# Two VectorE steps of an attention-and-MLP kernel moved one unit later: the row sums of batch 2, and half of the last chunk's S2

## The chip, the cores and the metric

The kernel runs on one core of a Trainium2 chip. The metric is the time on the device in microseconds (us), lower is better. It is quoted as the median of repeated runs; besides, there is one execution recorded by the hardware profiler, from which all durations of single instructions come.

## The reference

Eight batches with eight heads, 576 rows and 64 columns each go through a linear attention, and its result, seen as 4608 tokens of 512 numbers, through a two-layer network with a SiLU between the layers:

```
q_s = softmax(q) over the 64 columns of each row
k_s = softmax(k) over the 576 rows
kv  = k_s^T v                      (64 x 64 for each head)
x   = q_s kv, heads side by side   (4608 x 512)
h   = x w_in                       (4608 x 2048)
out = (h * sigmoid(h)) w_out       (4608 x 512)
```

The row sum of exp(q) and the product with its reciprocal, "row sums" and "normalising" below, are the softmax of q.

## The kernel before, in words

**Tiling.** The tokens are cut into nine chunks of 512 (`TCH`), numbered t = 0 to 8, the batches into eight of 576, numbered b. Chunk 0 is done with plain products. From chunk 1 on, both layers are done by a Strassen-Winograd scheme with one level: seven products of half size in the order `ORDER` = 1, 2, 6, 5, 7, 4, 3 instead of eight, paid for with sums on VectorE. For the first layer `group` (line 363) does one of the seven for one half (g = 1 or 0) of the columns of `w_in`; its sums of the inputs are `xs_op` (L330, on the tokens) and `ws_op` (L320, on the weights, once). The products 1, 6, 7 and 4 go to PSUM bank pair 0, the products 2, 5 and 3 to another pair (6 in chunk 1, 2 later). ScalarE copies bank pair 0 into the SBUF tiles H0, H1, H2 (`group_snap`), VectorE adds the other pair to them (`group_add`, L354), and ScalarE takes the SiLU into `GT` (`group_silu`, L359). The sum of H0 belongs to product 2 and empties the pair that product 5 overwrites. The sum of H2 belongs to product 7; product 3 then adds to the same pair and so has to wait until that sum has read it. For the second layer `s_op` (L451) forms S1 to S4 from `GT`, and `t_op` (L461) forms T1 to T4 from `w_out` once; `prod` (L477) does the products. S2 is one of the operands of product 6, and S4 is formed from S2.

**Batches.** For batch b, ScalarE takes `exp_q` and `exp_k` (L108, L113), VectorE sums the rows and takes the reciprocals (`qsum`, L156 and L158), GpSimd multiplies (`qnorm`, L163) and casts v (`vcast`, L91). SP's DMA queue then transposes the normalised q (`q_transpose`, L173). TensorE forms kv (`kv`, L195), VectorE divides it (`kvcopy`, L206 and L208), and TensorE forms x for the chunk (`xt_mm`, L234). The batch has two halves of four heads, numbered cc.

**What sets the order.** The order is written out by hand. The list `units` holds pieces of TensorE's work; `plan(u, f)` puts a step f just before unit u, and steps of the same unit run in the order in which they were planned. The whole is issued as one sequence (L826), and each engine works off its own instructions in this order, each waiting for its operands. So a step that is moved by one unit moves on its engine past whatever that unit issues there.

**Around batch 2's row sums.** Unit numbers b1 + n count from `b1`, the first unit after chunk 0's first layer. Units b1+9 to b1+22 mix the seven products of chunk 1 and g = 1 with chunk 0's plain second layer (`mm2_plain`, L414): product 1, mm2, product 2, product 6, mm2, product 5, mm2, product 7, mm2, mm2, product 4, mm2, product 3, mm2. Then follow eight plain pieces of chunk 1's first layer (`mm1`, L285), among which kv and xt of batch 2 are placed. At b1+10 come the four `xs_op` with `ws_op(1, 0)` and `exp_q(2, 0)`; at b1+11 `qsum(2, 0, 0)`, `qsum(2, 0, 1)` and `qnorm(2, 0)`; at b1+13 `exp_q(2, 1)` and `ws_op(2, 0)`; at b1+14 `exp_k(2, 0)` and the row sums and normalising of the other half; at b1+17 `exp_k(2, 1)` and the two casts of v; at b1+18 `t_op(2)`; at b1+24 `t_op(4)` and `ws_op(3, 0)`; at b1+25 `kv_both(2)`. The row sums of half 0 thus stand on VectorE's queue ahead of the sum of H0.

**Around the last chunk.** Chunk 8's first layer takes 28 units that end at `begin[NCH]`, mixed with chunk 7's second layer; after them comes chunk 8's second layer alone. The unit `begin[NCH] - 7` is product 7 of group g = 0, whose VectorE work is the sum of H2. Ahead of it stand `s_op(7, 4)` and one half, four of the eight blocks, of chunk 8's S2. The other half of S2 is formed after `begin[NCH]`.

Of the kernel before, what the change touches and what calls it, by code (L numbers as in the profile page):

```python
# [17 lines left out]
def kernel(  # L18
# [9 lines left out]
    nc = tc.nc  # L28
# [12 lines left out]
    NCH = NT // TCH  # L41
# [60 lines left out]
    def half(t, cc):  # L102
        return t[:, :, cc * 128:(cc + 1) * 128].rearrange("p j (g d) -> p j g d", d=D)

    def exp_q(b, cc, g0=0, g1=2):
        if "eq" not in st[b]:
            st[b]["eq"] = ap.tile([128, J, NG * D], BF16, name="eq")
        nc.scalar.activation(  # L108
            out=half(st[b]["eq"], cc)[:, :, g0:g1], in_=jgd(b, "qt", cc)[:, :, g0:g1], func=ACT.Exp
        )  # L110
# [34 lines left out]
    def new_zq(b):  # L145
        if "zq" not in st[b]:
            st[b]["zq"] = ap.tile([128, 2, J, 2], FP32, name="zq", bufs=2)
            st[b]["rzq"] = ap.tile([128, 2, J, 2], FP32, name="rzq", bufs=2)

    def qsum(b, cc, gs=None):  # L150
        new_zq(b)
        z, e = st[b]["zq"][:, cc], half(st[b]["eq"], cc)
        if gs is None:
            nc.vector.reduce_sum(out=z, in_=e, axis=AX.X)  # L154
        else:
            nc.vector.reduce_sum(out=z[:, :, gs], in_=e[:, :, gs, :], axis=AX.X)  # L156
        if gs != 0:
            nc.vector.reciprocal(out=st[b]["rzq"][:, cc], in_=z)  # L158

    def qnorm(b, cc, eng):  # L160
        e = half(st[b]["eq"], cc)
        r = st[b]["rzq"][:, cc]
        eng.tensor_tensor(  # L163
            out=e, in0=e, in1=r[:, :, :, None].to_broadcast([128, J, 2, D]), op=ALU.mult
        )
# [273 lines left out]
    def blk(t, kh, th):  # L439
        return GTS[t % 2][:, kh * HF:(kh + 1) * HF, th * HT:(th + 1) * HT]  # L440

    def s_op(t, i, f0=0, f1=HF):
        in0, in1, op = {
            1: (blk(t, 0, 1), blk(t, 1, 1), ALU.add),
            2: (SS[1], blk(t, 0, 0), ALU.subtract),
            3: (blk(t, 0, 0), blk(t, 0, 1), ALU.subtract),
            4: (blk(t, 1, 0), SS[2], ALU.subtract),
        }[i]
        f = slice(f0, f1)
        o = blk(t, 0, 1) if i == 3 else SS[i]  # L450
        nc.vector.tensor_tensor(out=o[:, f], in0=in0[:, f], in1=in1[:, f], op=op)  # L451
# [171 lines left out]
    def plan(u, f):  # L623
        at.setdefault(u, []).append(f)
# [7 lines left out]
    begin = {1: len(units)}  # L632
# [83 lines left out]
    begin[NCH] = len(units)  # L716
    last = NCH - 1
    plan(begin[NCH] - 11, lambda: s_op(last, 1, 4, 8))
    plan(begin[NCH] - 7, lambda: s_op(last, 2, 4, 8))
    plan(begin[NCH], lambda: (s_op(last, 1, 0, 4), s_op(last, 2, 0, 4), s_op(last, 3)))  # L720
    plan(begin[NCH] + 6, lambda: s_op(last, 4))

# [48 lines left out]
    b1 = begin[1]  # L771
# [26 lines left out]
    plan(b1 + 10, lambda: (xs_op(1, 1), ws_op(1, 0)))  # L798
    plan(b1 + 10, lambda: (xs_op(1, 2), xs_op(1, 3), xs_op(1, 4)))
    plan(b1 + 10, lambda: exp_q(2, 0))  # L800
    plan(b1 + 11, lambda: (qsum(2, 0, 0), qsum(2, 0, 1), qnorm(2, 0, nc.gpsimd)))
    plan(b1 + 13, lambda: exp_q(2, 1))
    plan(b1 + 14, lambda: exp_k(2, 0))
    plan(b1 + 14, lambda: (qsum(2, 1, 0), qsum(2, 1, 1), qnorm(2, 1, nc.gpsimd)))
# [56 lines left out]
```

## Time and profile before

| | |
|---|---|
| median of 14 runs | 263.47 us (262.94 to 264.06) |
| the profiled execution, its own time | 262.99 us |
| span in the profile | 261.2 us (1.79 us lie around it) |
| VectorE busy | 208.8 us (80%) |
| ScalarE busy | 187.6 us (72%) |
| GpSimd busy | 65.6 us (25%) |
| granted TensorE clock | 0.995 of full |

Lines as "L355" are lines of the kernel; h is one of H0 to H2, WS what `ws_op` forms, T what `t_op` forms, S what `s_op` forms, zq the row sums, rzq their reciprocals, eq the exponentials of q, PS the PSUM. In a timeline each line has the start, the length, the engine, the line with its operation, what it writes and reads, and in brackets how long the engine had been idle and what ended that. PE is TensorE, PEld its weight load, DVE VectorE, ACT ScalarE, POOL GpSimd.

A group of four mm2 matmuls takes the place of about 0.86 us on TensorE and one product of chunk 1 about 0.77 us, as their starts follow on each other. On VectorE, a sum h of chunk 1 takes 1.03 us, a `ws_op` 0.68 us, a half `s_op` 0.69 us and a `t_op` 1.22 us, each when nothing holds it up; the two row sums of one half take 1.41 us together and the reciprocal 0.27 us. On GpSimd one `qnorm` takes 2.11 us and one cast 1.15 us.

### The profile page before, as it was taken

The page shows a single profiled execution, that of the slowest core. Times are in us where ns is not written, and L with a number is a line of the kernel's source. Part 1 is how long each engine was busy: PE and PEld are TensorE (multiplying, and loading weights), DVE is VectorE, ACT ScalarE, POOL GpSimd, SP SyncE. Part 2 cuts the span into 40 slices and gives each one's busy share as a digit, 9 for nine tenths or more (in the row PEclk, how much of TensorE's full clock was granted, in tenths as well). Part 3 has the DMA queues.
Part 4 walks back from the last instruction along what each step waited for, and adds up shares of the span by engine and source line. Part 5 has one row for each costly group of instructions (what it writes and reads, how often), then busy time and mean ns, then how long its engine had stood idle before and what let it go on. Part 6 is the DMA issues. An engine that isn't in the chain of part 4 may idle for free.

```text
span 261.2 us, 6409 instructions
## 1 busy us (share of the span) xinstructions
PE 252.0 (96%) x2732; PEld 203.5 (78%) x2732; DVE 208.8 (80%) x268; ACT 187.6 (72%) x212; POOL 65.6 (25%) x63
## 2 busy tenths in 40 slices
PE   8899999799999999999999999999999999999992
PEld 3467656556888888888888888888888888888881
DVE  2867897998997999799979997999798548855832
ACT  4767977798994799479957995799573848484610
POOL 1663790460360306030603060306000000000003
PEclk9999999999999999999999999999999999999998
DMA  6999999669999586957694869530433003300624
GB/s 233 345 198 297 298 319 335 252 124 385 312 342 216 143 231 211 214 141 204 240 250 104 218 228 210 142 84 3 90 81 82 3 0 83 80 3 1 141 63 121
DMA packets 35964, 45.89 MB, mean 176 GB/s; under 512 B 16208, under 2 KB 21008, under 8 KB 35936
## 3 DMA queue, kind: packets, MB, share of 16 engines
q1 hardware_dynamic: 29568, 33.69, 47.3%
q0 software_dynamic: 6128, 11.60, 17.1%
q8 instruction: 21, 0.34, 0.5%
q10 hardware_dynamic: 240, 0.20, 0.2%
q14 instruction: 7, 0.06, 0.1%
HBM read 36.70 MB, written 9.44 MB: 177 GB/s over the span
## 4 chain that ended last, share of the span: by engine, by line
PE 84%; DMA 5%; issue 4%; POOL 2%; ACT 2%; DVE 2%; POOLq 0%; ACTq 0%
PE PS L477 37%; PE PS L377 34%; DMA qt<-in_q_dram 5%; PE PS L414 5%; PE PS L285 2%; PE PS L234 2%; PE PS L195 2%; POOL W L554 1%; PE PS L267 1%; POOL out_dram L740 1%; DVE zq L156 1%; ACT sg L256 0%; ACT eq L108 0%; PE PS L181 0%; DVE h L355 0%
## 5 line engine op out<-in xcount | busy, mean ns | idle before, releaser
L355 DVE TENSOR_TENSOR h<-PS,h 128x1024 f32<-128x1024 f32 (+1 forms) x45 | 53.9, 1198 | 12.2 <-ACT h L89 6.3
L477 PEld LDWEIGHTS <-GT 128*128 128x128 f16 x512 | 49.6, 98 | 6.9 <-issue 1.2
L377 PEld LDWEIGHTS <-WS 128*128 128x128 f16 x480 | 46.8, 98 | 7.9 <-issue 2.3
L477 PE MATMUL PS<-W,GT 128*128 128x256 f16 x384 | 49.1, 273 | 0.0
L377 PE MATMUL PS<-XS,WS 128*128 128x256 f16 (+1 forms) x360 | 46.3, 272 | 1.5 <-DVE h L355 1.5
L361 ACT ACTIVATE GT<-h 128x1024 f16<-128x1024 f32 (+1 forms) x45 | 46.1, 1047 | 0.3 <-DVE h L355 0.3
L89 ACT COPY h<-PS 128x1024 f32<-128x1024 f32 (+1 forms) x35 | 35.1, 1004 | 14.5 <-PE PS L377 14.1
L163 POOL TENSOR_TENSOR eq<-eq,rzq 128x1152 bf16<-128x1152 bf16 x13 | 27.5, 2117 | 55.2 <-DVE rzq L158 52.4
L477 PEld LDWEIGHTS <-S 128*128 128x128 f16 x384 | 37.2, 98 | 5.2 <-issue 1.0
L377 PEld LDWEIGHTS <-W 128*128 128x128 f16 x360 | 34.7, 98 | 4.7 <-issue 0.2
L477 PE MATMUL PS<-T,S 128*128 128x256 f16 x256 | 32.7, 273 | 0.0
L377 PE MATMUL PS<-XT,W 128*128 128x256 f16 (+1 forms) x240 | 29.5, 272 | 0.0
L361 ACT ACTIVATE GT<-PS 128x1024 f16<-128x1024 f32 (+1 forms) x15 | 15.3, 1017 | 18.9 <-PE PS L377 18.9
L91 POOL CAST vaug<-vt 128x1152 bf16<-128x1152 f32 x12 | 14.8, 1240 | 43.8 <-DMA vt<-in_v_dram 35.4
L108 ACT ACTIVATE eq<-qt 128x1152 bf16<-128x1152 f32 (+1 forms) x18 | 19.1, 1059 | 2.8 <-DMA qt<-in_q_dram 2.6
L740 POOL DMA_DIRECT2D out_dram<-ow x5 | 2.7, 546 | 72.5 <-DVE ow L725 72.5
L113 ACT ACTIVATE ek<-kt 128x1152 bf16<-128x1152 f32 x16 | 18.4, 1154 | 1.5 <-DMA kt<-in_k_dram 1.5
L154 DVE TENSOR_REDUCE zq<-eq 128x18 f32<-128x1152 bf16 x12 | 16.1, 1345 | 4.0 <-ACT eq L108 4.0
L477 PE MATMUL PS<-W,S 128*128 128x256 f16 x128 | 16.5, 273 | 0.0
L497 DVE SCALAR_TENSOR_TENSOR ow<-PS,sc 128x512 f32<-128x512 f32 x7 | 4.8, 692 | 14.5 <-ACT sc L493 14.5
L267 PE MATMUL PS<-XT,W 128*128 128x288 f16 x128 | 16.0, 286 | 0.1
L414 PE MATMUL PS<-W,GT 128*128 128x512 f16 x64 | 15.6, 379 | 0.0
(79 smaller groups left out, 345.2 us busy)
## 6 DMA issues: line engine op xcount, KB each, us to landing
out_dram<-ow SPq DMA_DIRECT2D x64, 128.0 KB, 2.4
qt<-in_q_dram SPq DMA_DIRECT2D x12, 576.0 KB, 4.6
kt<-in_k_dram SPq DMA_DIRECT2D x12, 576.0 KB, 5.4
vt<-in_v_dram SPq DMA_DIRECT2D x12, 576.0 KB, 5.4
qt<-in_q_dram POOLq DMA_DIRECT2D x4, 576.0 KB, 10.2
kt<-in_k_dram POOLq DMA_DIRECT2D x4, 576.0 KB, 13.5
vt<-in_v_dram POOLq DMA_DIRECT2D x4, 576.0 KB, 13.0
W<-in_moe_w_out_dram POOLq DMA_DIRECT2D x4, 512.0 KB, 14.6
```

The costliest lines, as they stand in the source:

```text
L89: eng.copy(out=o, in_=i)
L91: eng.tensor_copy(o, i)
L108: nc.scalar.activation(out=half(st[b]["eq"], cc)[:, :, g0:g1], in_=jgd(b, "qt", cc)[:, :, g0:g1], func=ACT.Exp)
L113: nc.scalar.activation(out=half(ek, cc), in_=jgd(b, "kt", cc), func=ACT.Exp)
L154: nc.vector.reduce_sum(out=z, in_=e, axis=AX.X)
L163: eng.tensor_tensor(out=e, in0=e, in1=r[:, :, :, None].to_broadcast([128, J, 2, D]), op=ALU.mult)
L267: nc.tensor.matmul(out=PS[:, WIDE[fb] + n, 0:S // 2], lhsT=W1[:, c, fb * 128:(fb + 1) * 128], rhs=XTS[0][:, c, n * (S // 2):(n + 1) * (S / ...
L355: nc.vector.tensor_tensor(out=four(t, i), in0=group_bank(t, True), in1=four(t, i), op=ALU.add)
L361: nc.scalar.activation(out=group_out(t, f, n), in_=x, func=ACT.Silu, scale=1.0 / XS)
L377: nc.tensor.matmul(out=PS[:, bank + p // 2, (p % 2) * HT:(p % 2) * HT + width(t)], lhsT=a[:, c, p * 128:(p + 1) * 128], rhs=bb[:, c, 0:wid ...
L414: nc.tensor.matmul(out=PS[:, 2 + tb, :], lhsT=GTS[t % 2][:, fc, tb * 128:(tb + 1) * 128], rhs=W2[:, fc, :], start=(fc == 0), stop=(fc == N ...
L477: nc.tensor.matmul(out=PS[:, bank, m * HN:(m + 1) * HN], lhsT=a[:, fc, m * 128:(m + 1) * 128], rhs=bb[:, fc, :], start=(first and fc == 0) ...
```

## The change

Both edits change one number, the unit ahead of which a step stands.

```diff
-    plan(begin[NCH] - 7, lambda: s_op(last, 2, 4, 8))
+    plan(begin[NCH] - 6, lambda: s_op(last, 2, 4, 8))
...
-    plan(b1 + 11, lambda: (qsum(2, 0, 0), qsum(2, 0, 1), qnorm(2, 0, nc.gpsimd)))
+    plan(b1 + 12, lambda: (qsum(2, 0, 0), qsum(2, 0, 1), qnorm(2, 0, nc.gpsimd)))
```

In the second edit the two row sums and the reciprocal of batch 2's half 0 go on VectorE's queue from before the sum of H0 (product 2, unit b1+11) to behind it. `qnorm(2, 0)` moves with them, but unit b1+11 issues nothing on GpSimd. In the first edit half of chunk 8's S2 goes from before the sum of H2 (product 7) to behind it. No instruction is added or removed, and no DMA is moved.

## Prediction

> **What bounds the kernel now.** First the page's busy times, then TensorE's waits, then the engines' busy time by stretches (columns: length, then busy us of PE, PEld, DVE, ACT, POOL, granted clock, DMA share, GB/s).
>
> ```profile
> PE 252.0 (96%) x2732; PEld 203.5 (78%) x2732; DVE 208.8 (80%) x268; ACT 187.6 (72%) x212; POOL 65.6 (25%) x63
> ```
> ```profile
> PE PS L377 <- DVE h L355: 1.5, 1, 1.5
> ```
> ```profile
> 41.80:48.00 6.20, 4.66 (x41) 3.54 (x38) 4.79 (x10) 5.60 (x6) 1.25 (x1) 1.00 1.11 337
> 48.00:62.70 14.70, 14.70 (x170) 8.45 (x168) 14.53 (x18) 11.81 (x17) 6.17 (x4) 1.00 0.70 208
> ...
> 219.90:243.70 23.80, 23.76 (x218) 21.14 (x217) 16.14 (x20) 15.53 (x18) 0.00 (x0) 1.00 0.18 40
> ```
>
> TensorE bounds. The one wait of over 1.2 us that it has is for a sum h; it lies between 41.8 and 48, where 1.54 us of 6.20 are idle. Behind it TensorE has no gap that I can find up to 241.8, so a us saved at 46 is kept to the end unless something else comes late. In 48 to 62.7, however, VectorE is busy 14.53 of 14.70: that is what will come late.
>
> The chain of waits says who makes the sum late:
>
> ```profile
> 43.65 1.18 ACT eq L108
> 44.83 0.02 issue
> 44.85 1.43 DVE zq L156 x2
> 46.27 0.02 issue
> 46.30 0.27 DVE rzq L158
> 46.56 0.96 DVE h L355
> 47.52 0.04 issue
> 47.56 0.93 PE PS L377 x8
> ```
>
> VectorE stands 0.98 us for the exponential, sums rows, takes the reciprocal, and only then adds H0, though product 2 had ended at 44.39 and ScalarE's copy of H0 at 43.76. TensorE's product 5 waits for this.
>
> **The first edit in time: the row sums.** With the sum of H0 first, it starts 0.04 behind product 2's end (the sum at 243.06 starts 0.04 after its product's end at 243.02): 44.43, and ends at 45.46. Product 5 follows four mm2 matmuls that start at 44.99, and such a group takes 0.86 of TensorE (52.45 to 53.31), so it is due at 45.85, not 47.56. **The stall is worth 47.56 - 45.85 = 1.71 us**; the sum has 0.39 to spare.
>
> What is late next? TensorE is now 1.71 ahead, and whatever it meets must be too. These rows of the timeline decide (VectorE and GpSimd; left-out rows are marked), with one from the view of the tile vaug (shortest, median and longest duration in ns):
>
> ```profile
> 46.48 1.03 DVE L355 TENSOR_TENSOR h<-PS,h 128x896 f32<-128x896 f32 x1
> 46.75 2.11 POOL L163 TENSOR_TENSOR eq<-eq,rzq 128x1152 bf16<-128x1152 bf16 x1 [7.26 <-DVE rzq L158]
> ...
> 47.42 1.98 DVE L328 TENSOR_TENSOR WS<-WS,W 128x1024 f16<-128x1024 f16 x1
> ...
> 51.09 1.09 DVE L355 TENSOR_TENSOR h<-PS,h 128x896 f32<-128x896 f32 x1
> 51.17 2.12 POOL L163 TENSOR_TENSOR eq<-eq,rzq 128x1152 bf16<-128x1152 bf16 x1 [2.32 <-ACT h L89]
> ...
> 52.10 2.27 DVE L461 TENSOR_TENSOR T<-W,T 128x2048 f16<-128x2048 f16 x1
> ```
> ```profile
> L91 POOL CAST vaug<-vt x2: 1153/1652/2152, 53.2 to 55.3; 128x1152 bf16<-128x1152 f32 x2
> ```
>
> The ws_op at 47.42 took 1.98 instead of 0.69: it ended at 49.40, that is 0.54 after GpSimd's normalising had ended at 48.86. The t_op at 52.10 took 2.27 instead of 1.22, ending 1.08 after the next normalising. The other way round, the first cast of v took 2.15 instead of 1.15: it had started behind that t_op and ended 1.01 after it. The sum h at 51.09, with one operand in PSUM, took 1.09 beside GpSimd, so it is not held. So the two engines exclude each other in operations that read two SBUF operands, and the first to start wins. The Trainium skill says so too and speaks against the change (SBUF — State Buffer, section SBUF: two separate sides: a pair of ports shared by VectorE and GpSimd is an exclusive lock, kept for the whole instruction): the edit puts ws_op(2, 0) directly behind the reciprocal that releases GpSimd's normalising. The sum depends on who is first.
>
> VectorE's queue after the edit: sum of H0 44.43; row sums from 45.37 (+0.94, as from 46.48 to 47.42; their exponential ended at 44.82); reciprocal 46.82 to 47.09 (+1.45, as 44.85 to 46.30). The next instruction starts 0.18 after a reciprocal's start (46.30 to 46.48), and GpSimd 0.45 after it (46.30 to 46.75). So ws_op starts at 47.00, GpSimd would at 47.27. Here a rule is less kind than the row: VectorE: DVE Perf Modes, section The DRAIN you can't avoid, lets the next operation start only when the pipe is empty, at 47.09 then. By the row VectorE leads by 0.27, by the rule by 0.18. I take VectorE first.
>
> Case A, VectorE first: ws_op 47.00 to 47.69; normalising ends 49.7 (ws_op's end, plus 2.11, less some 0.14 of start-up as with the cast). Second row sums 47.6 to 49.04, reciprocal to 49.34. Product 7 now starts at 47.48 and ends at 48.41; ScalarE has its exponential done at 48.40 and copies H2 to 49.36. Sum of H2 49.40 to 50.48; product 3, which needs it, is due at 53.31 - 1.71 = 51.60: no stall. Second normalising 49.65 to 51.77; t_op(2), queued at 50.41, is held to 51.77 + 1.08 = 52.85. The casts come behind it: 53.86 and 54.95. kv is due at 56.55 - 1.71 = 54.84, its second half, which needs the second cast, at 55.20: no stall. Sum of H1 to 53.85, an output copy to 54.46, t_op(4) queued at 54.37 and held by the second cast to 54.95 + 1.08 = 56.03; ws_op(3, 0) from 55.95, kvcopy's reciprocal 0.60 later at 56.55, its products end at 57.24 (58.09 to 58.78 before); xt can start 0.12 later as before (58.78 to 58.90): 57.36. It is due at 58.90 - 1.71 = 57.19. **So 0.17 is given back.** Covers: kt's second half lands 11.7 after its issue at 36.9, at 48.6, its exponential starts at 49.25; the v halves land at 50.15 and 51.66, before their casts; the transpose is issued at 51.8, lands 4.7 later at 56.5, due 57.19. ScalarE's table load and SiLU follow that exponential 1.7 earlier than before. If these covers were gone, each us of lateness would cost at most itself, less the margin (0.6 for kt).
>
> First edit: 1.71 - 0.17 = **1.54 gained**. Bounds of the unknown, who gets the ports: 1.71 gained if nothing comes late, 0.57 lost if GpSimd is first (below).
>
> **The second edit: half of S2.** Near the end:
>
> ```profile
> 240.11 0.69 DVE L451 TENSOR_TENSOR S<-S,GT 128x1024 f16<-128x1024 f16 x1
> 240.72 1.22 DVE L355 TENSOR_TENSOR h<-PS,h 128x1024 f32<-128x1024 f32 x1
> 240.81 0.86 PEld L477 LDWEIGHTS <-S 128*128 128x128 f16 x8
> 240.91 1.04 PE L477 MATMUL PS<-W,S 128*128 128x256 f16 x8
> ...
> 241.99 1.03 PE L377 MATMUL PS<-XT,WS 128*128 128x256 f16 x8
> ```
>
> Products follow each other by 0.87 here, so product 3 was due at 240.91 + 0.87 = 241.78 and came at 241.99, 0.05 after the sum of H2 had ended at 241.94. Without the half S2 the sum starts at 240.11 and ends at 241.33: **0.21 gained**. Behind it the half S2 runs 241.25 to 241.94, and the next on the queue, the output copy that started at 241.85, starts where it did. S2 is first read by product 6 at 247.22: 5 us of cover. The SiLU of H2 starts at 242.03, when ScalarE is free, so it gains nothing and hides nothing; the SiLU of H1, which had 0.29 idle ahead of it, can follow 0.21 earlier. If the cover failed, it would cost at most the half's own 0.69. GpSimd is idle in this stretch. The tail follows TensorE.
>
> **Sum.** 1.54 + 0.21 = 1.75. From the profiled execution's 262.99: 261.24 (span 259.45). The median shown is 0.48 above that execution, so **263.47 - 1.75 = 261.72**.
>
> **Rivals.**
> *B, GpSimd first (ends slower).* One mechanism, at 47.0: the normalising takes the ports before ws_op. It decides as soon as VectorE's lead of 0.18 to 0.27 is gone. Then normalising 47.27 to 49.38, ws_op held to 49.92, second row sums and reciprocal to 51.55, sum of H2 51.46 to 52.55: product 3, due 51.60, stalls 0.99. Second normalising 51.73 to 53.84, t_op(2) to 54.92, casts to 55.93 and 57.05, t_op(4) to 58.13, kvcopy to 59.35, xt at 59.47, against 58.90 before: 0.57 lost, 0.21 gained at the end, 263.83. For it: the row of 1.98. Against: there GpSimd had started 0.67 earlier, here it has not.
> *C, a part comes late.* The ports go first as in A, but once more an operation on the way to xt is held that I have free, or a landing slips. A hold costs its queue 1.0 to 1.3 (1.98 - 0.69, 2.27 - 1.22, 2.15 - 1.15); less what margin it meets, I put it at 0.4 to 1.15 on TensorE, 0.75 in the middle: 1.54 - 0.75 + 0.21 = 1.00, 262.47. For it: TensorE met kv at 56.55 when the last cast had just ended at 56.48, so margins are thin already. Against: worked through above, every landing and cast has its time.
> *D, the wait isn't what it seems.* If product 5 waited for something else as well, such as its weights, only 0.21 would stay: 263.26. Against: it started 0.05 after the sum's end, and one of its weight loads was done at 45.64.
>
> **How the numbers follow.** A 0.64, C 0.17, B 0.14, D 0.05. This kernel's measurement tells about 0.2%, 0.53 us, from no change. A and C lie beyond it; B's 0.36 lies within, but if its waits pile up it may pass 0.53, which takes a third of it; D lies within. So faster 0.80, same 0.15, slower 0.05. The range begins at the most that both stalls hold, 263.47 - 1.92 = 261.55, less 0.25 for the spread of medians: 261.3. It ends at C's worst, 1.75 - 1.15 = 0.60 gained, 262.9. B and D are outside.
>
> **What would show it.** The row sums' chain ahead of product 5 gone and product 5 at about 45.9: the first step. ws_op(2, 0) at 0.7 with the first normalising stretched: A; ws_op at about 2.9 and a stall ahead of product 3: B. xt of batch 2 at about 57.4, close behind kvcopy: the 0.17. Product 3 of the last group 0.87 behind its predecessor: the second edit. I am wrong if 41.8 to 63 loses what the first stall gave, above all through t_op held by casts, or if later chunks show new TensorE gaps.

## The result and the profile after

The changed kernel takes 261.72 us (median of 10 runs, 261.15 to 262.46) against 263.58 us for the kernel before (47 runs, 262.94 to 264.56): a ratio of 0.993, with a 95% interval of 0.9918 to 0.9942. The prediction was 1.75 us faster; the medians differ by 1.86.

The profiled execution after took 262.15 us (span 260.4), only 0.84 less than the one before. The rest was lost in its first 42 us, in which the change touches nothing: product 1 of chunk 1 starts at 42.78 where it started at 41.82 before. So the two traces are compared from that product on, and 0.96 is taken off each time of after that is set beside one of before.

The waits of TensorE after; the view lists those of more than 0.15 us:

```profile
PE PS L551 <- DVE XS L536: 1.2, 1, 1.2
PE PS L267 <- DVE GT L257: 0.8, 1, 0.8
PE PS L195 <- ACT vaug L89: 0.3, 1, 0.3
PE PS L267 <- DMA W<-in_moe_w_in_dram: 0.2, 1, 0.2
```

The wait for a sum h is gone. All four lie in the opening (L551 is the warm-up, L195 kv of batch 0, L267 chunk 0). Product 5 now follows the mm2 group ahead of it without a gap. First the two rows before, then after:

```profile
44.99 1.03 PE L414 MATMUL PS<-W,GT 128*128 128x512 f16 x4
47.56 0.93 PE L377 MATMUL PS<-XS,WS 128*128 128x224 f16 x8 [1.54 <-DVE h L355]
```
```profile
45.95 1.03 PE L414 MATMUL PS<-W,GT 128*128 128x512 f16 x4
46.82 0.93 PE L377 MATMUL PS<-XS,WS 128*128 128x224 f16 x8
```

The stretches after, in the same columns as in the prediction and in the trace's own time, that is, not shifted by 0.96:

```profile
41.80:48.00 6.20, 6.16 (x49) 4.37 (x48) 4.85 (x10) 5.33 (x6) 0.00 (x0) 1.00 1.11 337
48.00:62.70 14.70, 14.62 (x169) 8.52 (x168) 14.51 (x21) 13.16 (x20) 7.61 (x4) 1.00 0.74 228
...
219.90:243.70 23.80, 23.80 (x220) 21.32 (x218) 16.25 (x20) 15.46 (x18) 0.00 (x0) 1.00 0.19 41
```

TensorE's 1.54 idle us in the first have become 0.04; in their place 0.08 appear in the second, the first trace of what is late next. The chain of waits names it (start, length, what):

```profile
45.46 1.09 DVE h L355
46.55 1.33 DVE zq L156 x2
47.88 0.02 issue
47.91 0.27 DVE rzq L158
48.17 0.54 DVE WS L328
48.72 1.33 DVE zq L156 x2
...
51.36 2.48 DVE T L461
53.84 1.00 DVE h L355
54.84 0.60 DVE ow L429
55.44 1.60 DVE T L461
57.04 0.60 DVE WS L328
...
58.31 0.41 PE PS L234 x8
```

Before, the chain was on VectorE from 44.85 to 47.52 only and ran along TensorE behind that. Now it stays on VectorE for 13 us, up to kvcopy and xt of batch 2: TensorE is ahead of VectorE, and VectorE's queue sets when xt starts. Xt comes 1.77 behind the mm1 piece ahead of it, where it came 1.62 behind (57.28, 58.90) before:

```profile
56.54 1.69 PE L285 MATMUL PS<-XT,W 128*128 128x448 f16 x8
58.31 0.41 PE L234 MATMUL PS<-qT,kvn 64*64 64x128 bf16 x8
```

Who gets the shared ports is seen in the timeline and in the view of the tile eq (shortest, median, longest in ns):

```profile
48.09 0.63 DVE L328 TENSOR_TENSOR WS<-WS,W 128x1024 f16<-128x1024 f16 x1
...
48.35 4.41 POOL L163 TENSOR_TENSOR eq<-eq,rzq 128x1152 bf16<-128x1152 bf16 x2 [7.91 <-DVE rzq L158]
```
```profile
L163 POOL TENSOR_TENSOR eq<-eq,rzq x2: 2110/2221/2332, 48.4 to 50.6; 128x1152 bf16<-128x1152 bf16 x2
```

The weight sum that took 1.98 us before takes 0.63; the first normalising takes 2.33 instead of 2.11, since it waits for it. That is case A of the prediction. And the end:

```profile
239.39 1.22 DVE L355 TENSOR_TENSOR h<-PS,h 128x1024 f32<-128x1024 f32 x1
...
240.32 1.04 PE L477 MATMUL PS<-W,S 128*128 128x256 f16 x8
...
240.53 0.68 DVE L451 TENSOR_TENSOR S<-S,GT 128x1024 f16<-128x1024 f16 x1
...
241.19 1.04 PE L377 MATMUL PS<-XT,WS 128*128 128x256 f16 x8
```

Product 3 now follows its predecessor by 0.87 instead of 1.08, and the half S2 runs behind the sum of H2.

### The profile page after: what moved, and what is told of

Same layout as the page of the kernel before. It is cut to its first block, busy times and chain, and to the rows that moved or that the text cites. A ratio compares the mean times of both kernels' runs of the same rounds, so it can differ in the third digit from the quotient of the medians.

```text
span 260.4 us, 6411 instructions
## 1 busy us (share of the span) xinstructions
PE 252.4 (97%) x2732; PEld 203.7 (78%) x2732; DVE 207.7 (80%) x268; ACT 187.4 (72%) x212; POOL 65.8 (25%) x63
## 4 chain that ended last, share of the span: by engine, by line
PE 81%; DMA 5%; DVE 5%; issue 4%; POOL 2%; ACT 1%; POOLq 0%; ACTq 0%; DVEq 0%
PE PS L477 37%; PE PS L377 34%; DMA qt<-in_q_dram 5%; PE PS L414 3%; PE PS L234 2%; PE PS L195 2%; DVE T L461 2%; POOL W L554 1%; PE PS L285 1%; PE PS L267 1%; DVE zq L156 1%; DVE h L355 1%; POOL out_dram L740 1%; ACT sg L256 0%; DVE WS L328 0%
## 5 line engine op out<-in xcount | busy, mean ns | idle before, releaser
L377 PEld LDWEIGHTS <-W 128*128 128x128 f16 x360 | 34.7, 98 | 4.8 <-issue 0.2
L267 PE MATMUL PS<-XT,W 128*128 128x288 f16 x128 | 16.2, 286 | 0.9 <-DVE GT L257 0.8
L267 PEld LDWEIGHTS <-W 128*128 128x128 f16 x128 | 12.4, 98 | 4.7 <-issue 1.2
```

Of the source, the lines that this page charges most:

```text
L267: nc.tensor.matmul(out=PS[:, WIDE[fb] + n, 0:S // 2], lhsT=W1[:, c, fb * 128:(fb + 1) * 128], rhs=XTS[0][:, c, n * (S // 2):(n + 1) * (S / ...
L377: nc.tensor.matmul(out=PS[:, bank + p // 2, (p % 2) * HT:(p % 2) * HT + width(t)], lhsT=a[:, c, p * 128:(p + 1) * 128], rhs=bb[:, c, 0:wid ...
```

## The experiments

Ten kernels were run. Since the opening of a run varies, each was judged by its time and by one stretch of its trace: from the start of product 1 of chunk 1 to the start of chunk 2's first product. The edits lie in it, except that of S2 and the later places in e8. Each ratio is taken against runs of the kernel before that were made alongside. The quoted texts were written before the run.

| kernel | product 1 | chunk 2 | stretch | ratio to before, 95% interval |
|---|---|---|---|---|
| before | 41.82 | 62.73 | 20.91 | |
| after | 42.78 | 62.14 | 19.36 | 0.9930 (0.9918 to 0.9942) |
| e1, row sums only | 42.80 | 62.16 | 19.36 | 0.9941 (0.9927 to 0.9955) |
| e2, S2 only | 41.74 | 62.65 | 20.91 | 1.0001 (0.9988 to 1.0013) |
| e6, one row sum ahead | 41.61 | 61.62 | 20.01 | 0.9957 (0.9940 to 0.9973) |
| e3, clearing ahead of ws_op | 42.48 | 62.39 | 19.91 | 0.9947 (0.9928 to 0.9965) |
| e4, clearing behind ws_op | 42.12 | 61.80 | 19.68 | 0.9957 (0.9942 to 0.9973) |
| e11, one sum ahead of ws_op | 41.80 | 63.29 | 21.49 | 1.0018 (1.0011 to 1.0026) |
| e9, two sums ahead of ws_op | 42.02 | 63.51 | 21.49 | 1.0016 (1.0005 to 1.0028) |
| e10, two sums behind ws_op | 42.01 | 62.52 | 20.51 | 0.9971 (0.9960 to 0.9982) |
| e5, T4 behind kvcopy | 42.06 | 62.05 | 19.99 | 0.9952 (0.9936 to 0.9967) |
| e8, T4 into chunk 2 | 43.06 | 62.27 | 19.21 | 0.9929 (0.9908 to 0.9949) |

Behind this stretch little differs: from chunk 2's first product to the last chunk's second layer (at 243.73 before) TensorE takes 181.00 before and 181.02 in e1, and 180.79 to 180.83 in the kernels in which S2 is moved. Only e9 does not fit, with 181.00: one product of chunk 2 (at 81.15) comes 0.2 late there.

The theory: the sum of H0 was late by what stood ahead of it, behind the edit VectorE's queue decides, and in this queue who first takes the ports shared with GpSimd. The rivals were B (GpSimd first), and that the gain lies elsewhere (D of the prediction among them).

**The edits alone (e1, e2).** Each leaves the other as it was before.

```diff
 e1:  plan(begin[NCH] - 7, lambda: s_op(last, 2, 4, 8))      (as before)
 e2:  plan(b1 + 11, lambda: (qsum(2, 0, 0), ...))            (as before)
```

> Only the row sums are moved; half of S2 stays. Theory (each edit removes its own stall, and behind it VectorE's queue up to xt of batch 2 gives 0.17 back): 1.54 us faster than before (ratio 0.994); product 5 of chunk 1 0.86 behind the mm2 group ahead of it, xt of batch 2 about 0.15 later than due, product 3 of the last group still 1.08 behind its predecessor. Rival (the gain of 1.9 comes mostly from the last chunk, or the two edits help only together): less than 0.8 us.

> Only half of S2 is moved; the row sums stay. Theory: 0.21 us faster (ratio 0.9992, within what the times can tell, so the profile decides): product 3 of the last group 0.87 behind its predecessor instead of 1.08, the stall ahead of product 5 of chunk 1 unchanged at 1.71. Rival (the half S2 is only pushed in front of something else that is late): the 0.21 turns up again behind it, as a gap among the products of the last chunk's second layer.

e1 has the whole 1.55 of the stretch and, near the end, product 3 still 1.07 behind its predecessor (240.37, 241.44). e2 has a stretch as before, with product 5 waiting 1.54, and product 3 at 0.87 (240.83, 241.70). From chunk 2's first product to the last chunk's second layer it takes 243.45 - 62.65 = 180.80 against 243.73 - 62.73 = 181.00 before, and from there to VectorE's last instruction 12.43 in both. The 0.2 is kept and turns up nowhere as a gap. The time of e2 cannot tell 0.2 us from nothing; only the trace shows it. The edits are independent, and D has fallen: with the row sums moved, product 5 waits for nothing else.

**How much must move (e6).** One of the two row sums goes back ahead of the sum of H0.

```diff
-    plan(b1 + 12, lambda: (qsum(2, 0, 0), qsum(2, 0, 1), qnorm(2, 0, nc.gpsimd)))
+    plan(b1 + 11, lambda: qsum(2, 0, 0))
+    plan(b1 + 12, lambda: (qsum(2, 0, 1), qnorm(2, 0, nc.gpsimd)))
```

> The changed kernel with one of the two row sums of half 0 put back ahead of the sum of H0; the other, the reciprocal and the normalising stay behind it. Theory (product 5 waits exactly for what stands on VectorE's queue ahead of that sum): the exponential ends 0.4 behind product 2, one row sum takes 0.70 more, so the sum of H0 starts 1.1 behind product 2's end and product 5 comes 1.66 behind the mm2 group ahead of it, a stall of 0.80 instead of 1.71; behind it VectorE is only 0.4 later than in the changed kernel while TensorE is 0.8 later, so xt of batch 2 waits no more. 0.91 + 0.21 = 1.1 us faster than before. Rival (what counts is the whole length of VectorE's queue, not its order): the same as the changed kernel, 1.75 faster.

VectorE and TensorE of e6 in the timeline:

```profile
44.65 0.75 DVE L156 TENSOR_REDUCE zq<-eq 128x9 f32<-128x576 bf16 x1 [0.98 <-ACT eq L108]
45.31 1.08 DVE L355 TENSOR_TENSOR h<-PS,h 128x896 f32<-128x896 f32 x1
...
46.45 0.93 PE L377 MATMUL PS<-XS,WS 128*128 128x224 f16 x8 [0.64 <-DVE h L355]
```

Product 5 starts 1.66 behind the mm2 group at 44.79, as expected, and the stretch is 0.90 shorter than before (0.91 expected). The 1.71 us consist of two parts. With one row sum and the reciprocal behind it, the sum of H0 starts 0.66 behind the first row sum instead of 1.63, and 0.91 of this reach product 5. What is left, 0.80, is the row sum that still stands ahead (0.66) and the wait for the exponential, for which it starts 0.47 behind product 2's end (44.18). From their sum some 0.3 go off, by which the sum of H0 may be late before product 5 waits: in after it starts 0.11 behind product 2's end and is done 0.27 ahead of product 5. So of VectorE's 0.98 of standing less than half counts; the rest lies ahead of product 2's end. So it is the order ahead of this sum that counts, not the length of the queue.

**Who gets the ports (e3, e4).** A needless clearing of 1024 half-precision numbers per partition in a tile that is written later, ahead of or behind ws_op(2, 0).

```diff
 e3: +    plan(b1 + 12, lambda: nc.vector.memset(SS[4][:, 0:4], 0.0))
 e4: -    plan(b1 + 13, lambda: ws_op(2, 0))
     +    plan(b1 + 13, lambda: (ws_op(2, 0), nc.vector.memset(SS[4][:, 0:4], 0.0)))
```

> The changed kernel with one needless VectorE clearing of 1024 half-precision numbers per partition [...], put between the reciprocal of batch 2's first row sums and ws_op(2, 0), so that GpSimd's normalising starts first. Theory (the first of the two to start shuts the other out): ws_op held till the normalising's end plus 0.54, about 2.3 us long; product 3 of chunk 1 stalls about 1.1; xt of batch 2 about 2.25 later against product 1 of chunk 1 than in the changed kernel; all in all 0.5 us slower than before, 2.25 slower than the changed kernel. Rival (the clearing only costs its own time on a full VectorE): the same as the kernel with the clearing behind ws_op, that is 1.3 us faster than before.

> The changed kernel with the same needless clearing [...] directly behind ws_op(2, 0): VectorE has the same work more, but ws_op still starts before GpSimd's normalising. Theory: the second normalising and all behind it 0.42 later, xt of batch 2 0.57 later than due; 1.3 us faster than before, 0.4 slower than the changed kernel. Rival (VectorE has slack of half a us here): no loss against the changed kernel, 1.75 faster than before.

e3 missed. VectorE and GpSimd of e3, and its view of the tile eq:

```profile
47.93 0.48 DVE L802 MEMSET S<- 128x512 uint32 x1
48.33 0.63 DVE L328 TENSOR_TENSOR WS<-WS,W 128x1024 f16<-128x1024 f16 x1
...
48.06 4.95 POOL L163 TENSOR_TENSOR eq<-eq,rzq 128x1152 bf16<-128x1152 bf16 x2 [7.91 <-DVE rzq L158]
```
```profile
L163 POOL TENSOR_TENSOR eq<-eq,rzq x2: 2108/2490/2872, 48.1 to 50.9; 128x1152 bf16<-128x1152 bf16 x2
```

The clearing took 0.48 and moved ws_op by 0.54: ws_op starts 5.85 behind product 1, in after 5.31. The normalising has its recorded start 0.27 ahead of ws_op, and ws_op still ran in 0.63, while the first normalising took 2.87. The stretch grew by 0.55 over the changed kernel, not by 2.25. So either a recorded start of GpSimd is not the moment at which it takes the ports, or the clearing itself kept it out. e4 came out as expected but for 0.1: its stretch is 0.32 longer than that of after. It bears on the second of the two:

```profile
48.12 0.48 DVE L816 MEMSET S<- 128x512 uint32 x1
...
47.70 2.33 POOL L163 TENSOR_TENSOR eq<-eq,rzq 128x1152 bf16<-128x1152 bf16 x1 [7.60 <-DVE rzq L158]
```

Here the clearing lies within the normalising, ran its 0.48 all the same, and did not delay it: the normalising ended 1.97 behind ws_op's end (48.06), in after 1.96.

**The same with a tool that needs no shared port (e9, e10, e11).** Instead of the clearing, row sums over 576 weights, written into row sums that are formed later anyway. In after two row sums (48.63 to 50.03) took their usual 1.40 within the first normalising.

```diff
+    def pad(n):
+        for i in range(n):
+            w = W1[:, i, 0:J * D].rearrange("p (j d) -> p j d", d=D)
+            nc.vector.reduce_sum(out=st[2]["zq"][:, 1, :, i], in_=w, axis=AX.X)
...
 e9:  +    plan(b1 + 12, lambda: pad(2))
 e10: -    plan(b1 + 13, lambda: ws_op(2, 0))
      +    plan(b1 + 13, lambda: (ws_op(2, 0), pad(2)))
 e11: +    plan(b1 + 12, lambda: pad(1))
```

> The clearing was a bad tool: it gave GpSimd's normalising a lead of only 0.27 us, and ws_op still ran in 0.63. Now the changed kernel with two needless row sums over 576 weights (0.70 us each, one SBUF input, the form that ran beside GpSimd unhindered) between the reciprocal and ws_op(2, 0): ws_op comes to the head of VectorE's queue about 1.1 us after the normalising's start. Theory (the first to start shuts the other out, with a start-up of GpSimd of under 0.67): ws_op is held to 0.54 behind the normalising's end, about 1.5 us long; the stretch from product 1 of chunk 1 to chunk 2's first product is 21.6 us (19.36 in the changed kernel, 20.91 before), 0.5 slower than before in all. Rival (VectorE always wins against a normalising, and the 1.98 of before had another cause): ws_op 0.63 to 0.69 long, the stretch about 20.8.

> The changed kernel with the same two needless row sums directly behind ws_op(2, 0). Theory: ws_op 0.63 long and ahead of the normalising, VectorE's queue 1.4 longer; the stretch from product 1 of chunk 1 to chunk 2's first product 1.3 us longer than in the changed kernel, 20.7; 0.4 faster than before in all. It is about 0.9 shorter than with the sums ahead of ws_op, which is what the order of the ports alone is worth. Rival (no such order): the same as with the sums ahead.

> The changed kernel with one needless row sum (0.70 us) between the reciprocal and ws_op(2, 0): GpSimd's normalising starts about 0.4 ahead of ws_op's turn, between the 0.27 at which VectorE still went first and the 0.67 of before, at which GpSimd did. Theory (GpSimd takes the ports a fixed time after its recorded start; from the 0.14 of start-up seen at the casts I would say GpSimd is first here): ws_op about 2.2 long, the stretch from product 1 to chunk 2's first product 21.6. Rival (the start-up is over 0.4): ws_op 0.63, the stretch 20.4.

First e11, then e10, then e9, in the timelines of VectorE and GpSimd (e11 with a row of TensorE):

```profile
47.10 0.70 DVE L774 TENSOR_REDUCE zq<-W 128x9 f32<-128x576 f16 x1
47.71 2.32 DVE L328 TENSOR_TENSOR WS<-WS,W 128x1024 f16<-128x1024 f16 x1
...
47.37 2.11 POOL L163 TENSOR_TENSOR eq<-eq,rzq 128x1152 bf16<-128x1152 bf16 x1 [7.81 <-DVE rzq L158]
...
52.65 0.93 PE L377 MATMUL PS<-XT,WS 128*128 128x224 f16 x8 [0.90 <-DVE h L355]
```
```profile
47.32 0.63 DVE L328 TENSOR_TENSOR WS<-WS,W 128x1024 f16<-128x1024 f16 x1
47.86 1.40 DVE L774 TENSOR_REDUCE zq<-W 128x9 f32<-128x576 f16 x2
...
47.58 2.33 POOL L163 TENSOR_TENSOR eq<-eq,rzq 128x1152 bf16<-128x1152 bf16 x1 [7.91 <-DVE rzq L158]
```
```profile
48.59 1.66 DVE L328 TENSOR_TENSOR WS<-WS,W 128x1024 f16<-128x1024 f16 x1
...
47.59 2.11 POOL L163 TENSOR_TENSOR eq<-eq,rzq 128x1152 bf16<-128x1152 bf16 x1 [7.75 <-DVE rzq L158]
```

With GpSimd 0.34 ahead, ws_op is held to 0.55 behind the normalising's end, product 3 waits 0.90 for the sum of H2 and the second half of kv 0.62 for its cast. One row sum of 0.70 us costs 2.13 us of the stretch: more than the edit had gained, and the kernel is slower than before. That is what rival B describes. Twice as many row sums on the other side of ws_op (e10) cost 1.15. Two ahead of it (e9) cost the stretch no more than one, 2.13, since ws_op waits for the same end of the normalising, only shorter (1.66 us). The order at the ports alone is worth 21.49 - 20.51 = 0.98 us between e9 and e10, which do the same work; their medians, 263.65 and 262.57, agree.

**What is late next (e5, e8).** T4 and the third weight sum, held by a cast ahead of kvcopy, are moved behind kvcopy (e5) or into idle stretches of VectorE in chunk 2 (e8).

```diff
-    plan(b1 + 24, lambda: (t_op(4, nc.vector), ws_op(3, 0)))
 e5: -    plan(b1 + 25, lambda: kv_both(2))
     +    plan(b1 + 25, lambda: (kv_both(2), t_op(4, nc.vector), ws_op(3, 0)))
 e8: +    plan(begin[2], lambda: ws_op(3, 0))
     +    plan(begin[2] + 19, lambda: t_op(4, nc.vector))
```

> The changed kernel with T4 and the third weight sum, which stand ahead of batch 2's kvcopy on VectorE, put directly behind it. Theory (VectorE is full from 45 to 60, so an order within this stretch only moves the stall): xt of batch 2 comes on time (0.15 gained), but VectorE's copy of its result starts some 0.9 later, and the second xt waits for its PSUM banks about 0.8: 0.6 to 0.8 us slower than the changed kernel, 1.1 faster than before. Rival (the 0.15 is due to the held T4 alone): 0.15 faster than the changed kernel.

> The changed kernel with the third weight sum put behind the token sums of chunk 2, and T4 behind S4 of chunk 1, into stretches of 1.0 and 1.6 us in which VectorE stands idle in the changed kernel's profile. Theory: nothing of VectorE is late at xt of batch 2 any more, 0.15 us faster than the changed kernel, 1.9 faster than before; T4 is done about 0.8 ahead of product 4 of chunk 1, which reads it. Rival (T4 is late there): a gap ahead of product 4, no gain or a loss.

In both, xt of batch 2 follows its predecessor without delay (1.62 behind it, as before the change). In e8:

```profile
56.82 1.69 PE L285 MATMUL PS<-XT,W 128*128 128x448 f16 x8
58.44 0.41 PE L234 MATMUL PS<-qT,kvn 64*64 64x128 bf16 x8
```

In e5 the second xt then waits for VectorE's copy:

```profile
60.19 0.41 PE L234 MATMUL PS<-qT,kvn 64*64 64x128 bf16 x8 [0.71 <-DVE XT L91]
```

Its stretch is 0.63 longer than that of after. In e8 it is 0.15 shorter, and behind it TensorE takes 180.83, in after 180.80, so nothing is late there. This is the 0.15 that the change itself gave back. e8's time, 261.52 us, cannot be told from that of the changed kernel; it is the better one by its trace only.

## Why the prediction was right

Step by step, times of after less 0.96 beside those of the prediction:

- *The stall.* Product 5 at 45.86 (predicted 45.85). e1 and e6 show that what stood on VectorE ahead of the sum of H0 made it: without it the stall is gone, with one row sum of it put back 0.80 return. Right.
- *VectorE first at the ports.* ws_op at 47.13, 0.26 ahead of GpSimd's start (predicted 47.00, 0.27 ahead), and not held. Right. The prediction had also weighed a lead of 0.18, if VectorE's next operation waited for an empty pipe. The trace has ws_op 0.18 behind the start of the reciprocal, which takes 0.27, as the row had it; the section cited there itself says that an operation that is not held starts earlier.
- *The queue behind it.* First normalising ends at 49.72 (49.7), sum of H2 starts at 49.39 (49.40), second normalising ends at 51.80 (51.77), T2 done at 52.88 (52.85), casts done at 55.00 (54.95), T4 at 56.07 (56.03), kvcopy at 57.30 (57.24), xt at 57.35 (57.36).
- *What is given back.* xt is 0.15 later than due (0.17). The stretch is 1.55 shorter (1.54). e5 and e8 show that the cause is VectorE's queue: when T4 and a weight sum leave it, xt is on time.
- *Half of S2.* 0.21 at product 3; e2 shows that it is kept.
- *The sum.* 1.75 was predicted. In the traces it is 1.55 + 0.20 = 1.75; the medians say 1.86, with an interval of 0.6% to 0.8% of 263.58, 1.5 to 2.2 us. That the median is the predicted 261.72 to the last digit is luck: the median before had moved from 263.47 to 263.58 meanwhile, and the ten runs lie 1.3 us apart.

What was wrong is a term of rival B. I had it decide as soon as VectorE's lead of 0.18 to 0.27 was gone. If e3 is read as a matter of the ports, e3 and e11 put the point elsewhere: with GpSimd's start 0.27 ahead VectorE still went first, with 0.34 ahead GpSimd did. So the changed kernel is more than 0.5 us from that point, not 0.2, and I gave B, with 0.14, more than it deserved. Its price of 0.57 for the move of the row sums was right: e11's stretch is 21.49 - 20.91 = 0.58 longer than that of before. The needless row sum in it adds nothing, since ws_op waits for the normalising's end anyway. The reservation is that in e3 a clearing, not a row sum, stood in front; that it kept GpSimd out is unlikely after e4, but not excluded. The crossing is bracketed by two runs with different tools, not swept.

One reading of the prediction is too narrow: that the engines exclude each other in operations that read two SBUF operands. It holds for VectorE's side of these traces: ws_op and t_op were held, while the row sums, the clearing and the sums h with one operand in PSUM were not. On GpSimd's side the cast of v reads only one, and yet it was held by t_op (2.15 against 1.15 us) and held T4 (1.67 against 1.22 us, ending 1.08 behind the cast). The prediction's sums have the casts so, and came out.

Not tried: a later landing of kt or v, or of the transpose. In none of the profiled executions did one of them make TensorE wait in this stretch.

## What to carry to other kernels

Ahead of an operation that frees a PSUM bank on which TensorE waits, nothing that can wait should stand in the same queue, least of all what itself waits for another engine; find such a step in the chain of waits between TensorE and the operation. When such a step is moved, write the queue behind it out instruction by instruction until the waiting engine meets it again: here 1.71 us were freed and 0.15 given back, 11 us later. Where a step that releases GpSimd comes to stand next to VectorE work with two SBUF operands, look who starts first by their recorded starts, and count on neither where GpSimd leads by some tenths of a us: 0.27 and 0.34 fell on different sides here.

## What was not expected of the hardware

GpSimd's recorded start seems not yet to be its hold on the ports. The Trainium skill (SBUF — State Buffer, section SBUF: two separate sides) lets whichever starts first have them for the whole instruction; by recorded starts that failed at a lead of 0.27 (e3) and held at 0.34 (e11), so the measured starts decide only with an offset of about 0.3 us, if e3's clearing had no part in it.

The start of product 1 lies between 41.61 and 43.06 in these twelve traces, though the kernels are the same up to there, while the stretch behind it repeats: 21.49 in e9 and in e11, 19.36 in after and in e1, 20.91 in before and in e2. Most of what one run differs from the next is made in the opening, where TensorE's waits change from trace to trace (0.8 us for `GT` of L257 in after, none listed in before); what makes it was not studied. A change of a few tenths of a us is judged by a stretch of the trace, not by the time.
